# Decay attention beside an FFN on one Trainium2 core: attention's steps in two turns of TensorE per batch, and an earlier, wider spread for one block

## The chip, the cores and the metric

One core of one Trainium2 chip runs the kernel. Its engines work at the same time, each through its own queue in order: TensorE (PE, with weight loads as PEld), VectorE (DVE), ScalarE (ACT), GpSimd (POOL) and SyncE (SP), which issues most DMAs. The metric is device time in microseconds (us), the median over runs.

## The reference

Three stages follow each other; everything is fp32.

```python
# attention with decay: batch 4, heads 8, 768 tokens, head size 48
for t in range(S):
    cur = einsum('bhd,bhe->bhde', u * k[t], v[t])
    y[t] = einsum('bhd,bhde->bhe', r[t], state + cur)
    state = w * state + einsum('bhd,bhe->bhde', k[t], v[t])
x = y as (3072 tokens, 384)
x = (silu(x @ w_gate) * (x @ w_val)) @ w_out          # first FFN, 1536 wide
h = x @ w_in                                          # second FFN, 2048 wide
out = (h * tanh(softplus(h))) @ w_out
```

## The kernel before, in words

The tokens are cut into six blocks j of 128 tokens per batch; a block holds 4 batches b, so 512 columns. Attention works on one (j, b) at a time in chunk form: scores inside the chunk (`at_scores`, L444), a mask copied into an SBUF tile on VectorE (`at_mask`, L451), the output from state and scores (`at_out`, L460 and L468), the sum with the token's own part (`at_y`, L489), the chunk's contribution to the state (`at_state`, L502), the addition into the state (`at_sum`, L518), and a transpose of the output into the FFN's layout (`at_flip`, L539), which ScalarE copies to the high part x_hi (L540) and VectorE subtracts for the low part x_lo (`at_low`, L544). Decay factors (`at_decay`, L392), key factors (`at_keys`, L434) and the own part (`at_own`, L417 to L426) are prepared one batch ahead, from block 2 on mostly by GpSimd.

Every FFN product is three matmuls of split operands (`product`, L227 to L229). A unit is one block times one 128-wide slice of the first FFN: nine matmuls for gate, nine for val and nine of out, which belong to the unit before. Units 0 to 13 alternate between blocks 0 and 1; 14 to 18 finish block 0, 19 to 23 block 1; from unit 24 on come blocks 2 to 5, twelve units each. A string of `UNITS` says in which order a unit is written: "gate", "val" and "out" are matmuls, "act" is ScalarE's silu, "mul" is VectorE's product (L618), "rest" is VectorE's low part g_lo (L626), "tick" is one step of splitting the stored weights (VectorE L144 to L163, the subtraction L185 on VectorE for weights below number 36 and on GpSimd above, ScalarE L136 and L179, SP's loads), and "fill" is a place for attention.

A `Filler` spreads a list of steps evenly over a number of such places; when the next one begins, what is left of the old one is done at once (`flush`). `beside` says at which unit which list begins: at 14 the keys of block 1, at 15 its state updates (8 steps over 8 places), at 19 (`ready`) the two steps of `NEXT` and the 22 of block 2 over 14 places, and at 24, 36 and 48 the 22 steps of blocks 3, 4 and 5 over 34 places. `STEPS` holds the five steps of a batch; the parts of a step are written one after the other into all queues. "back0" is the flip of the batch before, "low1" its low part, "load0" allocates and loads the batch after next. Ticks are handed out at 1.5 a unit in units 14 to 18, at 0 in 19 to 23 and at 1.3 from 24 until all weights are split.

PSUM tiles named "at" (scores, two of them; flip; out; state) take turns on three buffers. The scores, masks and outputs of blocks 0 and 1 are done ahead of unit 0 and the change doesn't touch them.

Of the kernel before, what the change touches and what calls it, by code (L numbers as in the profile page):

```python
# [38 lines left out]


STEPS = [
    "scores0 own0", "mask0 back0 own1", "out0 low1 decay0 own2", "y0 state0 decay1 keys0",
    "sum0 load0",
]
LAST = ["flip0", "low2"]

# [2 lines left out]
NEXT = [[(1, B - 1, "own0 own1 decay1")], [(1, B - 1, "own2 decay0 keys0")]]  # L49


UNITS = [
    "gate act val tick mul tick",
    "gate rest val act tick out mul tick",
    "gate tick rest val act fill tick out mul",
    "gate rest fill act val mul tick out fill tick fill tick",
    "gate rest fill act val mul fill tick out fill tick tick",
]
# [4 lines left out]
PAIRED = 7  # L63
# [5 lines left out]
def tile_decay_attention_then_two_ffns(  # L69
# [31 lines left out]
    class Weights:  # L101
# [92 lines left out]
        def tick(self):  # L194
            n = self.at
            self.size(n + 2)
            self.bits(n)
            self.top(n)
            self.done(n - 2)

            self.load(n + 3)
            if n + 5 < 3 * NF1:
                self.load(n + 4)
                self.load(n + 5)
            self.at += 1
# [386 lines left out]
    def at_steps(j):  # L592

        return [[(j, b, step)] for b in range(B) for step in STEPS + LAST * (b + 1 == B)]
# [9 lines left out]
    def ffn1_mm(j, f, which):  # L604
        hi, lo = xs[j, "x"]
        ps = ps_mm.tile([P, NB], F32, name="mm")
        wt = weights.until((1, f, which))
        for c in range(KC):
            product(ps, wt, cols(c), hi[:, c, :], lo[:, c, :], c == 0, c == KC - 1)
        return ps  # L610

    def ffn1_act(ps):
        sg = opool.tile([P, NB], F32, name="o")
        nc.scalar.activation(sg, ps, AF.Silu)  # L614
        return sg

    def ffn1_gate(j, f, sg, ps):
        nc.vector.tensor_tensor(out=sg, in0=ps, in1=sg, op=ALU.mult)  # L618
        hi = gpool.tile([P, NB], F32R, name="g_hi")
        nc.scalar.activation(hi, sg, AF.Copy)  # L620
        gs[j, f] = [sg, hi]

    def ffn1_rest(j, f, eng):
        sg, hi = gs[j, f]
        lo = gpool.tile([P, NB], F32R, name="g_lo")
        eng.tensor_tensor(out=lo, in0=sg, in1=f32(hi), op=ALU.subtract)  # L626
        gs[j, f] = [hi, lo]

    def ffn1_out(j, f, first, last):
        acc = accs  # L630
        if (j, f) in BESIDE:

            acc = besides
        if first:
            for m in range(KC):
                if acc is besides:
                    acc[m] = ps_at.tile([P, NB], F32, name="at")
                else:
                    acc[m] = ps_acc.tile([P, NB], F32, name=f"acc{m}")
        hi, lo = gs.pop((j, f))  # L640
        wt = weights.until((1, f, 2))
        for m in range(KC):
            product(acc[m], wt, cols(m), hi, lo, first, last)
        if last:
            for m in range(KC):
                o = opool.tile([P, NB], F32, name="o")
                if m == 1:
                    nc.vector.tensor_copy(o, acc[m])
                else:
                    nc.scalar.activation(o, acc[m], AF.Copy)  # L650
                rows = mid[j][:, m * NB : (m + 1) * NB]
                if j in begun:
                    nc.gpsimd.dma_start(out=rows, in_=o, accum_op=ALU.add)
                else:
                    nc.sync.dma_start(out=rows, in_=o)
            begun.add(j)
# [79 lines left out]
    def ending():  # L736
        at_flip(*early[-1])
        at_low(*early[-1])

    def unit1(n, fill=nothing, tick=nothing):  # L740

        j, f, _, _ = units[n]
        gate = val = act = None
        for part in UNITS[n if n < 2 else 2 if n < 2 * PAIRED else 3 if n < 24 else 4].split():
            if part == "gate":
                gate = ffn1_mm(j, f, 0)
                if n == 0:
                    ending()
            elif part == "val":
                val = ffn1_mm(j, f, 1)  # L750
            elif part == "act":
                act = ffn1_act(gate)
            elif part == "mul":
                ffn1_gate(j, f, act, val)
            elif part == "rest" and n:
                ffn1_rest(*units[n - 1][:2], nc.vector)
            elif part == "out" and n:
                ffn1_out(*units[n - 1])
            elif part == "fill":
                fill()  # L760
            elif part == "tick":
                tick()
# [3 lines left out]
    ready = NF1 + PAIRED  # L766
    beside = {
        2 * PAIRED: (KEYS, 3),
        2 * PAIRED + 1: (STATES, 8),
        ready: (NEXT + at_steps(2), 14),  # L770
    }
    beside.update({12 * j - 12: (at_steps(j), 34) for j in range(3, NJ)})
    fill = Filler([], 1)
# [1 line left out]
    for n in range(len(units) - NF1):  # L775
        if n in beside:
            fill.flush()
            fill = Filler(*beside[n])
        due += 2 if n < 2 * PAIRED else 1.5 if n < ready else 0 if n < 24 else 1.3
        some = int(due) if weights.at < W_STORED + 2 else 0  # L780
        ticks = [weights.tick if i < some else nothing for i in range(3)]
        due -= int(due)
        turn = iter(ticks)
        unit1(n, fill, lambda: next(turn)())
# [33 lines left out]
    for f in range(NF1):  # L818
        unit1(len(units) - NF1 + f)
        if f == 2:  # L820
            load_mid(0)
        if f in (5, 6, 7):
            split_mid(0, f - 5)
        for n in range(3 if f else 0):
            weights.tick()
# [186 lines left out]
```

## Time and profile before

| | us |
|---|---|
| median of 3 runs | 957.14 (957.1 to 957.28) |
| profiled execution | 956.94 |
| its span | 955.2 |
| TensorE busy | 944.3 (99% of the span) |
| VectorE, ScalarE, GpSimd busy | 628.2, 473.8, 163.5 |

The busy times are shares of one span, added up over stages of different kinds. A timeline row gives the start of an operation (or of several merged ones, with their count), its length, engine, line and the tiles it writes and reads; in brackets stands how long the engine had been idle before it and what ended that. Matmuls overlap: the distance between two starts tells the time that one takes.

### The profile page before, as it was taken

How to read it: one execution, taken by the hardware profiler on the slowest of the kernel's cores; microseconds unless marked ns; L12 is line 12 of the kernel's file. 1: busy time of each engine (PE TensorE's matmuls, PEld its weight loads, DVE VectorE, ACT ScalarE, POOL GpSimd, SP SyncE). 2: the span in 40 equal slices, each digit the busy share in tenths (PEclk: the TensorE clock that was granted, in tenths of full speed). 3: DMA queues.
4: the chain of work that ended last, by engine and by line, in shares of the span. 5: the costliest groups of instructions: out<-in, count | busy, mean ns of one | idle time of the engine just before them, and what ended most of it. 6: DMA issues, size and time to landing. Idle time of an engine off the chain costs nothing.

```text
span 955.2 us, 14700 instructions
## 1 busy us (share of the span) xinstructions
PE 944.3 (99%) x5707; PEld 770.6 (81%) x5707; DVE 628.2 (66%) x1170; ACT 473.8 (50%) x841; POOL 163.5 (17%) x148
## 2 busy tenths in 40 slices
PE   8999999999999999999999999999999999999998
PEld 6778888787788787888888888888888888888886
DVE  8998868446765766533322249868678777787774
ACT  2455543323343433311221248867676776777673
POOL 5100001764654464322000000000000000000000
PEclk9999999999999999999999999999999999999999
DMA  8464432446646655230046630001001010000000
GB/s 324 176 195 133 132 101 66 128 128 173 218 148 208 217 164 192 92 103 1 1 165 198 197 102 22 12 26 41 1 34 34 0 47 21 1 34 1 33 1 34
DMA packets 35781, 93.17 MB, mean 98 GB/s; under 512 B 4224, under 2 KB 4352, under 8 KB 35712
## 3 DMA queue, kind: packets, MB, share of 16 engines
q1 hardware_dynamic: 35280, 91.44, 29.5%
q0 software_dynamic: 432, 0.79, 0.6%
q8 instruction: 45, 0.74, 0.3%
q14 instruction: 24, 0.20, 0.1%
HBM read 69.41 MB, written 22.81 MB: 97 GB/s over the span
## 4 chain that ended last, share of the span: by engine, by line
PE 87%; DVE 5%; DMA 4%; issue 2%; ACT 1%; POOL 1%; SPq 0%; DVEq 0%; POOLq 0%; ACTq 0%
PE mm L227 12%; PE mm L228 11%; PE mm L229 11%; PE acc L227 11%; PE acc L228 11%; PE acc L229 11%; PE at L228 5%; PE at L229 4%; PE at L227 4%; DMA w_split<-rk_t 2%; PE at L468 2%; PE at L444 2%; PE at L460 1%; DVE w_num L150 1%; DVE w_num L144 1%
## 5 line engine op out<-in xcount | busy, mean ns | idle before, releaser
L227 PE MATMUL mm<-x_hi,w_split 128*128 128x512 f32 x546 | 217.6, 398 | 0.0
L229 PE MATMUL mm<-x_hi,w_split 128*128 128x512 f32 x546 | 213.0, 390 | 0.0
L228 PE MATMUL mm<-x_lo,w_split 128*128 128x512 f32 x546 | 212.9, 390 | 0.0
L228 PE MATMUL acc<-g_lo,w_split 128*128 128x512 f32 x483 | 188.4, 390 | 0.8 <-DVE g_lo L626 0.7
L227 PE MATMUL acc<-g_hi,w_split 128*128 128x512 f32 x483 | 188.8, 391 | 0.0
L229 PE MATMUL acc<-g_hi,w_split 128*128 128x512 f32 x483 | 188.0, 389 | 0.0
L618 DVE TENSOR_TENSOR o<-mm,o 128x512 f32<-128x512 f32 x72 | 49.7, 691 | 192.4 <-PE mm L229 162.4
L227 PEld LDWEIGHTS mm<-x_hi,w_split 128*128 128x128 f32 x546 | 102.5, 188 | 22.7 <-DVE o L618 0.4
L229 PEld LDWEIGHTS mm<-x_hi,w_split 128*128 128x128 f32 x546 | 102.5, 188 | 21.8
L228 PEld LDWEIGHTS mm<-x_lo,w_split 128*128 128x128 f32 x546 | 102.6, 188 | 20.0
L620 ACT ACTIVATE g_hi<-o 128x512 fp32r<-128x512 f32 x72 | 45.5, 632 | 141.4 <-DVE o L618 141.1
L228 PEld LDWEIGHTS acc<-g_lo,w_split 128*128 128x128 f32 x483 | 90.7, 188 | 21.0 <-DVE g_lo L626 2.0
L227 PEld LDWEIGHTS acc<-g_hi,w_split 128*128 128x128 f32 x483 | 90.6, 188 | 19.2
L229 PEld LDWEIGHTS acc<-g_hi,w_split 128*128 128x128 f32 x483 | 90.7, 188 | 18.8
L614 ACT ACTIVATE o<-mm 128x512 f32<-128x512 f32 x72 | 42.8, 594 | 89.5 <-PE mm L229 82.4
L848 ACT ACTIVATE e<-h 128x512 f32<-128x512 f32 x96 | 60.0, 626 | 53.4 <-DVE h L842 50.4
L855 ACT ACTIVATE e<-e 128x512 f32<-128x512 f32 x96 | 59.6, 621 | 49.4 <-DVE e L852 49.3
L862 DVE TENSOR_TENSOR h<-h,e 128x512 f32<-128x512 f32 x96 | 60.0, 687 | 20.5 <-ACT e L861 20.5
L185 POOL TENSOR_TENSOR w_raw<-w_num,w_raw 128x384 fp32r<-128x384 f32 x32 | 40.9, 1279 | 160.4 <-ACT w_raw L179 158.3
L227 PE MATMUL at<-x_hi,w_split 128*128 128x512 f32 x174 | 67.7, 389 | 0.0
L228 PE MATMUL at<-x_lo,w_split 128*128 128x512 f32 x174 | 67.7, 389 | 0.0
L229 PE MATMUL at<-x_hi,w_split 128*128 128x512 f32 x174 | 67.7, 389 | 0.0
(105 smaller groups left out, 1347.6 us busy)
## 6 DMA issues: line engine op xcount, KB each, us to landing
w_raw<-w SPq DMA_DIRECT2D x68, 384.0 KB, 3.5
w2s<-w_raw SPq DMA_DIRECT2D x32, 384.0 KB, 3.7
w_split<-w2s SPq DMA_DIRECT2D x32, 384.0 KB, 3.5
n_sb<-rkv_n SPq DMA_DIRECT2D x16, 576.0 KB, 4.9
rk_sb<-rk_t SPq DMA_DIRECT2D x16, 512.0 KB, 4.5
mid<-o SPq DMA_DIRECT2D x18, 256.0 KB, 2.2
rows<-mid SPq DMA_DIRECT2D x18, 256.0 KB, 2.6
y<-o SPq DMA_DIRECT2D x18, 256.0 KB, 2.3
```

The lines of the kernel that those rows point to most:

```text
L185: eng.tensor_tensor(out=t[:, 1, :], in0=num, in1=f32(t[:, 0, :]), op=ALU.subtract)
L227: nc.tensor.matmul(acc, lhsT=wt[:, 0, sl], rhs=hi, start=start, stop=False)
L228: nc.tensor.matmul(acc, lhsT=wt[:, 0, sl], rhs=lo, start=False, stop=False)
L229: nc.tensor.matmul(acc, lhsT=wt[:, 1, sl], rhs=hi, start=False, stop=stop)
L444: nc.tensor.matmul(ps[g][:, i, :], lhsT=a["k"][q, i, :], rhs=a["r"][q, i, :], start=True, stop=True,)
L468: nc.tensor.matmul(ps[t, h * D : (h + 1) * D], lhsT=scores[h % 2][:, h // 2, t], rhs=a["v"][:, h, :], start=(j == 0 and h == heads[0]), st ...
L614: nc.scalar.activation(sg, ps, AF.Silu)
L618: nc.vector.tensor_tensor(out=sg, in0=ps, in1=sg, op=ALU.mult)
L620: nc.scalar.activation(hi, sg, AF.Copy)
L848: nc.scalar.activation(es[n], hs[n], AF.Exp)
L855: nc.scalar.activation(e, e, AF.Ln, bias=1.0)
L862: nc.vector.tensor_tensor(out=hs[n], in0=hs[n], in1=es[n], op=ALU.mult)
```

## The change

The five steps of a batch are cut anew: the flip of the batch before stands in front of the scores, the low part right behind the mask, the state update right behind the output, its sum behind y, and the load alone. Units 2 and 3 are written in the order that only unit 1 had. The list with block 2's steps begins at unit 17 instead of 19 and is spread over 20 places instead of 14.

```diff
 STEPS = [
-    "scores0 own0", "mask0 back0 own1", "out0 low1 decay0 own2", "y0 state0 decay1 keys0",
-    "sum0 load0",
+    "back0 scores0 own0", "mask0 low1 own1", "out0 state0 decay0 own2",
+    "y0 sum0 decay1 keys0", "load0",
 ]
 LAST = ["flip0", "low2"]
...
-        for part in UNITS[n if n < 2 else 2 if n < 2 * PAIRED else 3 if n < 24 else 4].split():
+        for part in UNITS[0 if n == 0 else 1 if n < 4 else 2 if n < 2 * PAIRED else 3 if n < 24 else 4].split():
...
-        ready: (NEXT + at_steps(2), 14),
+        ready - 2: (NEXT + at_steps(2), 20),
```

## Rows read from the trace of the kernel before

**Rows 1.** The page, part 1: busy us, share of the span, instructions.
```profile
PE 944.3 (99%) x5707; PEld 770.6 (81%) x5707; DVE 628.2 (66%) x1170; ACT 473.8 (50%) x841; POOL 163.5 (17%) x148
```

**Rows 2.** Waits of TensorE: us in total, times, longest us.
```profile
PE at L460 <- DVE s L451: 1.6, 4, 0.5
...
PE acc L228 <- DVE g_lo L626: 0.7, 1, 0.7
```

**Rows 3.** Timeline of VectorE in unit 2: start us, length us, operation.
```profile
58.38 0.35 DVE L144 TENSOR_SCALAR w_num<-w_num 128x384 f32<-128x384 f32 x1
...
60.32 0.68 DVE L626 TENSOR_TENSOR g_lo<-o,g_hi 128x512 fp32r<-128x512 f32 x1
```

**Rows 4.** Timeline of TensorE in unit 2, the out's first two matmuls.
```profile
60.05 0.39 PE L227 MATMUL at<-g_hi,w_split 128*128 128x512 f32 x1
61.06 0.50 PE L228 MATMUL at<-g_lo,w_split 128*128 128x512 f32 x1 [0.62 <-DVE g_lo L626]
```

**Rows 5.** TensorE, block 3: turns alone; the scores stand between the last two.
```profile
240.53 0.39 PE L229 MATMUL mm<-x_hi,w_split 128*128 128x512 f32 x1
240.84 0.88 PE L460 MATMUL at<-state,rk_sb 128*64 128x96 f32 x16
...
244.75 0.39 PE L227 MATMUL mm<-x_hi,w_split 128*128 128x512 f32 x1
...
246.88 0.56 PE L502 MATMUL at<-n_sb 128*48 128x48 f32 x16
...
249.55 0.39 PE L227 MATMUL acc<-g_hi,w_split 128*128 128x512 f32 x1
...
256.99 0.39 PE L227 MATMUL acc<-g_hi,w_split 128*128 128x512 f32 x1
```

**Rows 6.** TensorE, units 19 to 23 (attention of block 2), first and last.
```profile
163.84 0.39 PE L227 MATMUL mm<-x_hi,w_split 128*128 128x512 f32 x1
...
202.47 0.49 PE L539 MATMUL at<-ident,y 128*128 128x128 f32 x3
202.89 0.88 PE L460 MATMUL at<-state,rk_sb 128*64 128x96 f32 x16
...
206.95 0.40 PE L229 MATMUL mm<-x_hi,w_split 128*128 128x512 f32 x1
...
209.59 0.39 PE L227 MATMUL acc<-g_hi,w_split 128*128 128x512 f32 x1
...
211.63 0.39 PE L227 MATMUL mm<-x_hi,w_split 128*128 128x512 f32 x1
```

**Rows 7.** VectorE: a tick of unit 18, and one operation of another.
```profile
162.92 1.16 DVE L144 TENSOR_SCALAR w_num<-w_num 128x384 f32<-128x384 f32 x1
...
166.66 0.55 DVE L163 SCALAR_TENSOR_TENSOR w_num<-w_raw,w_num 128x384 uint32<-128x384 uint32 x1
...
284.05 0.55 DVE L150 SCALAR_TENSOR_TENSOR w_num<-w_raw,w_num 128x384 uint32<-128x384 uint32 x1
```

**Rows 8.** GpSimd beside the first of these ticks, and beside the other.
```profile
162.84 1.03 POOL L417 TENSOR_TENSOR pr<-n_sb 128x384 f32<-128x384 f32 x1
...
284.01 2.62 POOL L426 TENSOR_TENSOR n_sb<-n_sb,bonus 128x384 f32<-128x384 f32 x1 [4.37 <-DVE bonus L425]
```

**Rows 9.** VectorE by line, 170 to 212: busy us, mean ns, idle before.
```profile
L451 DVE COPY_PREDICATED s<-mask,at 128x512 f32<-128x512 uint16 x8 | 5.4, 731 | 6.2 <-PE at L444 6.2
...
L518 DVE TENSOR_TENSOR state<-at,state 48x192 f32<-48x192 f32 x8 | 2.8, 351 | 0.1
L618 DVE TENSOR_TENSOR o<-mm,o 128x512 f32<-128x512 f32 x4 | 2.8, 691 | 13.0 <-issue 6.9 <-PE mm L229 6.1
L489 DVE TENSOR_TENSOR y<-at,n_sb 128x384 f32<-128x384 f32 x4 | 2.2, 554 | 1.0 <-PE at L468 1.0
L544 DVE TENSOR_TENSOR x_lo<-at,x_hi 128x384 fp32r<-128x384 f32 x4 | 2.2, 544 | 0.9 <-ACT x_hi L540 0.9
```

**Rows 10.** TensorE, block 3's batch 2: one of the waits for the mask.
```profile
261.96 0.88 PE L460 MATMUL at<-state,rk_sb 128*64 128x96 f32 x16 [0.36 <-DVE s L451]
```

## The prediction

> **What bounds the kernel now.** I read the busy times first [rows 1]: TensorE is busy for 944.3 of 955.2 us, so the time moves only with what TensorE executes, what it pays for changing between kinds of matmul, and the few waits that it has. The list of its waits comes next [rows 2]; the reader is to see there that no wait on a DMA or on ScalarE is named, that attention's output matmuls (L460) wait four times for the mask, and that the FFN waits for a low part (g_lo). Last come the timelines: of TensorE for what one turn costs [rows 5, 6], of VectorE and GpSimd for how the two disturb each other [rows 7, 8]. The profiled execution took 956.94 us, 1.7 more than its span; it is 0.2 below the median, 957.14. The sum is made on 956.94.
>
> I call a stop of the FFN's matmuls for attention a turn. Nine FFN matmuls in a row take 2.04 (209.59 to 211.63 in [rows 6]), one 0.227. A turn costs what a stretch takes beyond its FFN matmuls.
>
> **Turns alone** [rows 5]: out (O) 244.75 - 240.53 less ten matmuls: 1.95. State (St) 4.80 less eighteen: 0.72. Scores (S) 7.44 less twenty-seven: 1.32. From [rows 6], flip (F) 209.59 - 206.95 less ten: 0.37.
>
> **Turns joined** [rows 6]: O and St back to back start at 202.89, and the eighth start after their first FFN matmul is 206.95: 4.06 less 1.81 is 2.25, with O's lead (240.84 - 240.53 - 0.23 = 0.08) 2.33, against 1.95 + 0.72 = 2.67. A join of O and St is worth 0.34. F followed by attention matmuls takes 0.42 (202.47 to 202.89), and F with S then 0.42 + 1.32 - 0.08 = 1.66 against 1.69: worth 0.03. So of the two joins only one pays. I take bounds of 0.2 to 0.4 and 0 to 0.2 for them.
>
> **Part 1, units 2 and 3 take UNITS[1].** In unit 2 a weight tick (VectorE 58.38 to 60.32, 1.94) stands ahead of the rest that makes g_lo [rows 3], and TensorE's second matmul of the out comes 1.01 after the first instead of 0.23 [rows 4]: 0.8. Behind the change the rest runs where that tick ran, done at about 59.0, before 60.05. The tick is not saved, it moves to the end of the unit: units 3 and 4 then have two ticks in a row ahead of unit 4's rest, some 2 us later than now; by adding the steps of 1.94 and 0.6 it is done at 71.5, its matmul due at 72.8, so nothing is late next. SP's loads and GpSimd have no other work there. -0.8 (bounds -1.0 and 0, if a later rest takes the wait over).
>
> **Part 2, the last state update of block 1.** The filler is flushed at unit 17, so the fourth state follows the third without FFN between: one lead and tail less, -0.2 (0 to -0.4). Its sum stands ahead of a rest that is not needed for 4 us.
>
> **Part 3, block 2.** The 24 steps now run at 14 places of units 19 to 23, 1.7 a place, so that several share a stop. Units 19 to 23 last 47.79 [rows 6], less 135 matmuls (30.6): 17.2 for turns and waits. With 20 places, step s stands at the first place n with 20 s < 24 n. Counted out: batch 0 has S in unit 17's second place, O with St in unit 18's first; batch 1 F with S in unit 18's third, O with St in unit 19's second; batch 2 F, S, mask and low in unit 20's second place and O with St in its third, with no FFN matmul between; batch 3 has two free turns; the last F is alone. Without waits but for batch 2: 1.32 + 2.33 + 1.66 + 2.33 + 1.66 + 2.33 + 0.37 = 12.0. Batch 2: out takes the third buffer of "at" after F's own, so it now waits until low has read F's, and low stands behind both masks: 0.42 + 1.10 + 1.3 + 0.5 + 0.1 + 2.25 = 5.7, with mask, low, sum, mul and y of 0.6 to 0.7 a half, 0.5, 0.7, 0.65 and 0.5 [rows 9]. Together 17.7, so +0.5: before, the mask, O and St shared a stop too.
>
> Then two waits that the start at unit 17 makes, since units 17 and 18 still carry three ticks (units 19 to 23 none).
> First: from the end of unit 17's val, VectorE has mul, tick, tick, mask: 0.6 + 1.94 + 1.94 + 1.3 = 5.8. TensorE has out, S, gate and the first half of O (some 0.7 of the 0.88 in [rows 10]): 2.04 + 1.32 + 2.04 + 0.7 = 6.1, and then needs the mask. That just fits, if a tick takes 1.94. GpSimd, however, gets from unit 17's first place the keys of batch 0 and own and decay of batch 1, whose data lie there since the front, and runs them without a gap. Where that was so, the four VectorE operations of a tick took from 162.92 to 167.2 [rows 7] beside GpSimd's stream [rows 8], 4.2 instead of 1.5: +2.7, so a wait of 2.4. From the other side, at 284.01 [rows 8] it was GpSimd's operation that took 2.62 instead of about 1, and VectorE's L150 beside it kept its 0.55 [rows 7]: a wait of 0. I take 2.3, because unit 17's tick meets a stream that already runs, as at 162.92. Behind the mask on VectorE stand rest and the bonus reduce; their users come later.
> The Trainium skill, page "SBUF — State Buffer", section "Who interferes with whom", says that issue order, not the shape of the operation, decides which of VectorE and GpSimd blocks. Both rows agree with that; by it the sum is 960.4 if GpSimd's stream is there first, 957.6 if the tick is (rival B).
> Second: in unit 18's third place F needs y, and S the buffer that sum gives back. y and sum were put in at the second place, behind mul and a tick: from val's end 0.65 + 1.5 + 0.5 + 0.7 = 3.4 until S may start, against out's 2.04 and F's 0.42. F waits 0.7, S 0.3: 1.0 at least, 1.9 with one GpSimd operation (0.9) in the tick. I take 1.5.
> Block 2: 0.5 + 2.3 + 1.5 = +4.3 (bounds 0.5 + 0 + 1.0 = +1.5 and 0.5 + 2.7 + 1.9 = +5.1).
>
> **Part 4, blocks 3 and 4** (22 steps over 34 places, the step of n at place 17 n / 11). O and St join, eight times. The price is the same buffer: O waits for low behind both masks, where it now waits for the first half of the mask: about 0.65 + 0.45 = 1.1 later wherever VectorE is behind. Of the four waits of [rows 2], one each lies in blocks 3 (261.96, [rows 10]) and 4. There the join saves nothing, as F's 0.37, which lay inside the wait, is now ahead of it: +1.1 each. In block 3, batch 0, sum (0.7) comes ahead of the ticks that already make out wait 0.7 for g_lo [rows 2]; the 0.34 of its join goes there: 0. Block 3: 0 - 0.37 + 1.1 - 0.37 = +0.3; block 4: three clean joins and one wait, 0. Bounds -1.5 and +1.5 each.
> Block 5 has no state: three joins of F, -0.1. The load alone in its step stays at its place; state is read earlier, so SP's two issues wait no longer. Low needs ScalarE's copy of F, a place earlier now: nothing.
>
> **Sum**: -0.8 - 0.2 + 4.3 + 0.3 + 0 - 0.1 = +3.5: 956.94 + 3.5 = **960.4 us**.
>
> **Rivals.**
> (A) Faster: VectorE is nowhere late. GpSimd gives way as at 284.01, and both waits of L460 in blocks 3 and 4 go, because the changed order shifts the ticks against GpSimd's stream. All joins then count: -0.8 - 0.2 + (0.5 + 0 + 1.0) - 1.45 - 1.45 - 0.1 = -2.5: 954.4. For it: the two waits are 0.36 and 0.5 long and two of eight. Against it: low adds 0.5 to the same queue. It decides if a tick in unit 17 stays under some 2.2 us.
> (B) GpSimd gives way in unit 17 alone: the first wait is 0 and the second 1.0: +0.7, 957.6.
> (C) Unit 17 waits as forecast, but blocks 3 and 4 are clean: 3.5 - 0.3 - 2.9 = +0.3, 957.2.
> (D) More waits than forecast: low takes another 1.1 in two of the six clean outs of blocks 3 and 4: 962.6.
>
> **How the numbers follow.** Forecast 0.35, D 0.1, B 0.2, C 0.13, A 0.22. A measurement of this kernel tells 0.2% (1.9 us) from nothing: faster is below 955.2, slower above 959.05. A is faster, B and C no change, the forecast and D slower: 0.22, 0.33, 0.45. The range, 954.4 to 962.6, reaches from A to D since both signs hold a good part; the forecast's own range is 958.8 to 961.8.
>
> **What would show it.** Unit 2's out without an idle before its second matmul (part 1). St right behind O in blocks 3 and 4, with 2.33 for both (joins). In unit 18 an L468 idle for the mask of about 2 us, VectorE's ticks before it drawn out to 4 us; an idle of L539 for y in unit 18's third place; an O in unit 20 that starts some 1.9 after S. In blocks 3 and 4 L460 waiting for x_lo (L544) instead of s (L451). If units 17 and 18 hold no idle on TensorE, the forecast is wrong in its largest term; if TensorE's joined turns take 2.67, the gain of the joins is.

## The result and the profile after

The changed kernel is slower: 963.79 us median of six runs (960.17 to 965.11), against 957.21 of six runs before on the same chip; ratio 1.0056, 95% interval 1.0040 to 1.0072. By this ratio the change costs 5.4 us; the two medians are 6.6 apart. The sign is that of the forecast (+3.5, 960.4), the median lies 1.2 above the range's upper end. The profiled execution is the slowest of the six, 965.11; its span is 963.4, 8.2 more than before.

The page's first part and TensorE's waits, which answer to [rows 1] and [rows 2]:

```profile
PE 946.0 (98%) x5707; PEld 776.1 (81%) x5707; DVE 632.2 (66%) x1170; ACT 474.0 (49%) x841; POOL 163.1 (17%) x148
```
```profile
PE at L460 <- DVE s L451: 3.3, 3, 1.7
PE at L468 <- DVE s L451: 2.6, 2, 2.3
PE at L539 <- DVE y L489: 2.5, 3, 1.4
PE mm L227 <- DVE o L618: 2.5, 1, 2.5
```

Two waits of over 2 us are new: L468 for the mask, and a val for VectorE's mul (L618). To place the time I use that mul runs once a unit, 72 times, so its n-th start marks unit n in every trace. The table gives what each stretch lasts more or less than before; "ahead" is the start of unit 0's first matmul against 44.75. Of the 8.2 us of the changed kernel's span 1.9 lie ahead, 6.1 in the units of the table and 0.2 behind them.

| us against before | ahead | units 0 to 13 | 13 to 24 (block 2) | 24 to 36 (block 3) | 36 to 48 (block 4) | 48 to 71 | sum without ahead |
|---|---|---|---|---|---|---|---|
| changed kernel | +1.91 | +2.82 | +5.56 | -1.75 | -0.40 | -0.12 | +6.11 |
| steps alone | +3.25 | 0.00 | +0.62 | -1.90 | -1.57 | -0.12 | -2.97 |
| units 2, 3 alone | +0.33 | -0.90 | +0.01 | +0.11 | -0.26 | +0.01 | -1.03 |
| places alone | +4.75 | +2.93 | +5.16 | -0.19 | -0.05 | 0.00 | +7.85 |
| late loads | -0.04 | -0.91 | +5.56 | -1.94 | -1.59 | -0.12 | +1.00 |
| small matmuls in the wait | +0.25 | +2.69 | +3.62 | -1.39 | -0.49 | -0.12 | +4.31 |
| ticks ahead | +0.05 | +3.14 | +3.24 | +0.23 | -2.21 | -0.12 | +4.28 |
| late loads and ticks ahead | +0.45 | -0.91 | +3.19 | -0.45 | -1.99 | -0.12 | -0.28 |
| steps and units | +1.61 | -0.88 | +0.67 | -1.19 | -1.58 | -0.12 | -3.10 |
| short preparation | +0.81 | +2.91 | +0.16 | -1.21 | -0.46 | -0.10 | +1.30 |
| steps from block 3 on, and units | +0.15 | -0.91 | +0.01 | -1.28 | -1.55 | -0.12 | -3.85 |

The column "ahead" lies in front of all that the change touches, and varies from one execution to the next: in the changed kernel's profile the granted clock was 0.69 between 15 and 20 us, in the profile before 1.00. Such an execution carries up to 4.75 us that no edit explains; the medians carry some of it too.

**What the front lost.** Timelines of the changed kernel around unit 1: GpSimd, VectorE, TensorE, and the windows (from the busy time of PE to its granted clock, the third number from the end).

```profile
50.46 1.02 POOL L417 TENSOR_TENSOR pr<-n_sb 128x384 f32<-128x384 f32 x1 [12.22 <-DMA n_sb<-rkv_n]
51.56 1.01 POOL L419 TENSOR_TENSOR pr<-pr,u_sb 128x384 f32<-128x384 f32 x1
52.52 1.59 POOL L392 TENSOR_TENSOR rk_sb<-rk_sb,tab 128x512 f32<-128x512 f32 x1
```
```profile
50.72 0.98 DVE L144 TENSOR_SCALAR w_num<-w_num 128x384 f32<-128x384 f32 x1
51.62 1.36 DVE L150 SCALAR_TENSOR_TENSOR w_num<-w_raw,w_num 128x384 uint32<-128x384 uint32 x1
52.91 1.62 DVE L185 TENSOR_TENSOR w_split<-w_num,w_split 128x384 fp32r<-128x384 f32 x1
...
55.19 0.68 DVE L618 TENSOR_TENSOR o<-mm,o 128x512 f32<-128x512 f32 x1
```
```profile
55.92 0.80 PE L227 MATMUL mm<-x_hi,w_split 128*128 128x512 f32 x1 [2.48 <-DVE o L618]
56.52 0.63 PE L228 MATMUL mm<-x_lo,w_split 128*128 128x512 f32 x1
56.94 0.63 PE L229 MATMUL mm<-x_hi,w_split 128*128 128x512 f32 x1
```
```profile
56.00:60.00 4.00, 4.00 (x11) 3.18 (x12) 4.00 (x11) 2.47 (x5) 0.00 (x0) 0.61 0.60 168
```

These three GpSimd operations prepare block 2. Before, they stood in GpSimd's queue behind its first weight subtraction, and ran when that did; GpSimd's timeline of before:

```profile
161.87 1.02 POOL L185 TENSOR_TENSOR w_raw<-w_num,w_raw 128x384 fp32r<-128x384 f32 x1 [125.54 <-ACT w_raw L179]
162.84 1.03 POOL L417 TENSOR_TENSOR pr<-n_sb 128x384 f32<-128x384 f32 x1
```

Written two units earlier, they come ahead of it. Nothing in the queue holds them any more, and they run when their data land, at 50 us, where VectorE is behind: its tick lasts from 50.72 to 55.19, 4.5 instead of 1.94 [rows 3]. mul of unit 0 is late, the next val waits 2.48 for the PSUM tile that mul frees, and its matmuls then start 0.43 apart, the lower of the clock's two levels (0.61 is the mean over 4 us), for 3.4 us. It is not the loads that draw out the tick: the kernel before issues them in the same place (43.2 and 44.2, 5.4 and 8.1 us to landing), and its tick at 48.81 takes 1.94.

**What block 2 lost.** The changed kernel's units 17 and 18: GpSimd, VectorE and TensorE, then a window.

```profile
161.37 1.13 POOL L417 TENSOR_TENSOR pr<-n_sb 128x384 f32<-128x384 f32 x1
162.57 1.20 POOL L419 TENSOR_TENSOR pr<-pr,u_sb 128x384 f32<-128x384 f32 x1
163.74 1.61 POOL L392 TENSOR_TENSOR rk_sb<-rk_sb,tab 128x512 f32<-128x512 f32 x1
```
```profile
160.89 0.74 DVE L144 TENSOR_SCALAR w_num<-w_num 128x384 f32<-128x384 f32 x1
...
165.95 0.34 DVE L144 TENSOR_SCALAR w_num<-w_num 128x384 f32<-128x384 f32 x1
...
167.90 1.32 DVE L451 COPY_PREDICATED s<-mask,at 128x512 f32<-128x512 uint16 x2
```
```profile
165.52 0.88 PE L460 MATMUL at<-state,rk_sb 128*64 128x96 f32 x16
168.66 1.95 PE L468 MATMUL at<-n_sb,s 128*64 128x48 f32 x32 [2.26 <-DVE s L451]
...
178.22 0.52 PE L539 MATMUL at<-ident,y 128*128 128x128 f32 x3 [0.80 <-DVE y L489]
```
```profile
168.00:176.00 8.00, 7.34 (x61) 6.26 (x62) 2.80 (x5) 2.06 (x6) 3.98 (x4) 0.57 0.15 57
```

The first tick takes 5.06 (160.89 to 165.95), the second 1.95, the mask is late and L468 waits 2.26: this is the forecast's first wait, to 0.04 of its size. The second is there too, 0.80. But behind the first the clock was at the lower level for 6.7 us (0.57 in the mean over 8 us), which the forecast did not have.

### The profile page after: what moved, and what is told of

Same layout as the page of the kernel before. It is cut to its first block, busy times and chain, and to the rows that moved or that the text cites. A ratio compares the mean times of both kernels' runs of the same rounds, so it can differ in the third digit from the quotient of the medians.

```text
span 963.4 us, 14692 instructions
## 1 busy us (share of the span) xinstructions
PE 946.0 (98%) x5707; PEld 776.1 (81%) x5707; DVE 632.2 (66%) x1170; ACT 474.0 (49%) x841; POOL 163.1 (17%) x148
## 4 chain that ended last, share of the span: by engine, by line
PE 89%; DVE 4%; DMA 2%; issue 1%; ACT 1%; POOL 0%; SPq 0%; DVEq 0%; POOLq 0%; ACTq 0%
PE mm L227 12%; PE mm L228 12%; PE mm L229 12%; PE acc L228 11%; PE acc L227 11%; PE acc L229 11%; PE at L229 4%; PE at L227 4%; PE at L228 4%; PE at L468 2%; PE at L444 1%; PE at L460 1%; DMA w_raw<-w 1%; PE at L539 1%; DVE w_num L150 1%
## 5 line engine op out<-in xcount | busy, mean ns | idle before, releaser
L618 DVE TENSOR_TENSOR o<-mm,o 128x512 f32<-128x512 f32 x72 | 49.7, 691 | 194.1 <-PE mm L229 165.3
L614 ACT ACTIVATE o<-mm 128x512 f32<-128x512 f32 x72 | 42.8, 594 | 97.1 <-PE mm L229 89.0
L876 DVE TENSOR_TENSOR g_lo<-h,g_hi 128x512 fp32r<-128x512 f32 x96 | 65.6, 686 | 2.2
```

Of the source, the lines that this page charges most:

```text
L876: nc.vector.tensor_tensor(out=lo, in0=h, in1=f32(hi), op=ALU.subtract)
```

## The experiments

Theory P, formed on the two traces: the early start of block 2's list costs everything, through GpSimd's preparation at 50 us and in units 17 and 18; the steps and the units gain. Its rival S: the closer order of mask, low, output and state costs.

**The three edits alone.** Each is one hunk of the diff above.

> The new steps alone, places and units as before. Theory P (the early start of block 2's list costs everything: GpSimd's preparation for block 2 becomes the first thing in its queue, runs at about 50 us beside the weight ticks, and again meets the ticks of units 17 and 18): faster, about 955.0 (957.2 less 1.8 in block 3 and 0.4 in block 4), no wait of TensorE over 1 us behind 45 us. Theory S (the closer order of mask, low, output and state makes TensorE wait): 959 or more, with waits of L460 or L468 over 1 us in units 19 to 23.

> The order of units 2 and 3 alone. Forecast's part 1: 956.4 (0.8 less), no wait for g_lo in unit 2. Rival (the wait moves to a later unit): 957.2 with a g_lo wait in unit 3 or 4.

> Block 2's list from unit 17 over 20 places alone, steps and units as before. Theory P: slower by 6 to 8, 963 to 965: a val in unit 1 waits 2 to 3 for its PSUM tile with the clock at its lower level behind it (3.6 together), and unit 18's output waits about 2 for the mask with the lower clock behind it. Theory S: within 1 of before, 956 to 958.

Steps alone: 956.78, ratio 0.9987 (0.9976 to 0.9997). Units alone: 956.53, 0.9985 (0.9971 to 0.9999), -0.90 in units 0 to 13 and no wait for g_lo there. Places alone: 964.21, 1.0072 (1.0051 to 1.0092), with the same two waits:

```profile
PE at L468 <- DVE s L451: 2.6, 2, 2.3
PE mm L227 <- DVE o L618: 2.5, 1, 2.5
```

S falls: with the old steps the places cost all of it, and the new steps gain. The steps' median gain, 0.6, is smaller than the 2.2 expected; the profile has 2.97 behind the first unit and +3.25 ahead of it, so most of the difference lies where the edit does nothing.

**Block 2's first loads later.** In the changed kernel the four DMAs that bring the data of block 2's first two batches are issued in front of unit 16.

```diff
-    for b in range(2):
-        at_tiles(EARLY, b)
-        load_at(EARLY, b)
...
     for n in range(len(units) - NF1):
...
+        if n == 16:
+            for b in range(2):
+                at_tiles(EARLY, b)
+                load_at(EARLY, b)
```

> The changed kernel with block 2's first two loads issued ahead of unit 16 instead of ahead of unit 0, so that GpSimd cannot begin at 50 us. Theory P: the wait near 55 us and the lower clock behind it go, 960.2 (963.8 less 3.6); the wait in unit 18 stays. Rival (the wait near 55 us comes from the new order of units 2 and 3 or from the weights' loads): the wait stays, 963.8.

959.86, ratio 1.0022 (1.0007 to 1.0037), 3.9 below the changed kernel: expected was 3.6. GpSimd now starts behind the DMA:

```profile
145.98 1.39 POOL L417 TENSOR_TENSOR pr<-n_sb 128x384 f32<-128x384 f32 x1 [109.71 <-DMA n_sb<-rkv_n]
```

Units 0 to 13 gain 0.91 instead of losing 2.82, and the windows at 50 to 60 us have the full clock. The front's loss is thus shown: 3.73 for the wait and the clock behind it.

Block 2 again costs 5.56, but that the sum is the same is chance. GpSimd's stream now covers the whole first tick of unit 17, which takes 6.31 (155.20 to 161.51), and the output waits longer:

```profile
164.22 1.28 PE L468 MATMUL at<-n_sb,s 128*64 128x48 f32 x32 [3.52 <-DVE s L451]
```

In return the clock is at the lower level for 3.4 us (165.4 to 168.8) instead of 6.7.

**TensorE kept busy in the wait.** Between the two halves of block 2's first output, 24 small matmuls write to the tile's unused columns; they disturb the sums of that tile, so this output is not the kernel's.

```diff
+WARM = 24
...
+        for _ in range(WARM if (j, b) == (EARLY, 0) else 0):
+            nc.tensor.matmul(ps[:, DM:], lhsT=mask, rhs=mask, start=True, stop=True, skip_group_check=True)
         heads = [*range(0, H, 2), *range(1, H, 2)]
```

> The changed kernel with 24 small matmuls on unused columns between the two halves of block 2's first output, where TensorE idles 2.3 for the mask. Theory C (the idle brings TensorE's clock to its lower level and that costs 3 more): the mask still comes at the same time, but the matmuls behind it run at 0.227 apart, about 961 (963.8 less 3). Rival (they are slow for another reason, or the clock falls in any case): 0.43 apart as before, 963.8 or more.

961.27, ratio 1.0035 (1.0023 to 1.0047). The timeline, L467 being the small matmuls, L471 the second half and L542 the next flip, and a window:

```profile
164.54 1.51 PE L467 MATMUL at<-mask 128*128 128x128 bf16 x24
166.86 1.29 PE L471 MATMUL at<-n_sb,s 128*64 128x48 f32 x32 [0.81 <-DVE s L452]
...
174.49 0.52 PE L542 MATMUL at<-ident,y 128*128 128x128 f32 x3 [1.67 <-DVE y L492]
```
```profile
166.00:174.00 8.00, 6.01 (x67) 4.75 (x66) 5.57 (x11) 3.22 (x9) 4.19 (x4) 1.00 0.15 59
```

The mask comes as late as it did, the clock stays at 1.00, and block 2 loses 3.62 instead of 5.56. So the lower clock cost block 2 1.9. By the rows alone it is 3.0 (in the changed kernel L468 and state took 2.52 and the nine FFN matmuls behind them 4.00; at batch 1's turn, 186.98 to 190.53, it was 1.38 and 2.17). Most of the difference comes back in the flip, which now waits 1.67 for y instead of 0.80.

**Ticks ahead of unit 17**, alone and with the late loads.

```diff
-        due += 2 if n < 2 * PAIRED else 1.5 if n < ready else 0 if n < 24 else 1.3
+        due += 2 if n < ready - 2 else 1 if n == ready - 2 else 0 if n < 24 else 1.3
```

> The changed kernel with the weight ticks of units 14 to 18 dealt out 2, 2, 2, 1, 0 instead of 1, 2, 1, 2, 1. Theory P (ticks of units 17 and 18 meet GpSimd's stream and hold mask and y back): the wait of L468 in unit 18 falls to 0.5 or less, the lower clock behind it and the flip's wait for y go, 958.5 to 959.5; the wait near 55 us stays. Rival (the mask is late because of the steps or of GpSimd itself): L468 waits 2 as before, 963.8.

> The changed kernel with the late loads and the ticks dealt out 2, 2, 2, 1, 0: both collisions away. Theory P: 954 to 956, since the steps and units then show their gain. Rival (GpSimd's work, now in units 15 and 16 beside two ticks each, makes a new wait there): 958 or more with a wait in units 15 to 17.

The first was a miss: 962.35, ratio 1.0043 (1.0020 to 1.0067). L468's wait fell to 0.3 and the flip's to 0.2, but others came instead:

```profile
PE mm L227 <- ACT o L614: 2.9, 2, 2.2
PE mm L227 <- DVE o L618: 2.6, 1, 2.6
PE acc L228 <- DVE g_lo L626: 2.5, 2, 2.1
```

The 2.1 (2.09 at 162.15, in unit 17's out) and another wait of 0.75 (155.47, unit 17's first matmul) lie where the moved ticks now stand: VectorE comes to its rest only behind two ticks and the sums, and ScalarE's L614 of unit 16 stands behind the tick's L179, which waited until L502 was done (154.40). The 2.2 lies elsewhere, at 236.28, the start of unit 26 in block 3: there ScalarE's L614 runs only at 235.63, behind a DMA from its buffer to mid. Why that came later than in the changed kernel was not followed.

With the late loads it is 959.84, ratio 1.0007 (0.9982 to 1.0033): no different from before, and above the 954 to 956 expected. The rival held here: the waits of 0.75 and 2.07 in unit 17 are there again (151.75 and 158.44), one of 1.51 at the start of unit 26 too, and block 2 again loses 3.19. In neither of the two spreads that were run do the seven ticks of units 14 to 18 fit beside block 2's early start.

**GpSimd's preparation cut short.** Batch 1's own part and decay and the last own operation of batch 0 work on a few columns only, so their results are left undone; the ticks stay.

```diff
+SHORT = {(2, 0, 2), *((2, 1, i) for i in (0, 1, 2, 4, 5))}
...
+        if (j, b, 4 + i) in SHORT:
+            eng.tensor_tensor(out=junk, in0=t[:, 0, :8], in1=tabs[i][:, 0, :8], op=ALU.mult)
...
+        n = 4 if (j, b, i) in SHORT else D
```

The last line is in `at_own`, whose operands are all cut to n of the 48 columns.

> The changed kernel with GpSimd's preparation for block 2's batch 1 (own part and decay, five operations) and the last own operation of batch 0 cut to a few columns each; their results are left undone. The ticks stay in units 17 and 18. Theory P (GpSimd's stream draws out the tick of unit 17 and so holds the mask): that tick takes about 2 instead of 4.6 us, L468 in unit 18 waits less than 0.5, the clock stays, and block 2 costs 3 to 5 less, 959 to 961. Rival (the two ticks and the mask are too much for VectorE without GpSimd): L468 waits 1 or more, 963.8 less at most 1.

958.48, ratio 1.0004 (0.9990 to 1.0019). VectorE's ticks and mask, and TensorE's output (L474 and L482 are its halves, L553 the flip):

```profile
159.87 0.35 DVE L145 TENSOR_SCALAR w_num<-w_num 128x384 f32<-128x384 f32 x1
...
161.88 0.34 DVE L145 TENSOR_SCALAR w_num<-w_num 128x384 f32<-128x384 f32 x1
...
163.83 1.35 DVE L465 COPY_PREDICATED s<-mask,at 128x512 f32<-128x512 uint16 x2
```
```profile
164.50 0.88 PE L474 MATMUL at<-state,rk_sb 128*64 128x96 f32 x16
165.21 1.09 PE L482 MATMUL at<-n_sb,s 128*64 128x48 f32 x32
...
171.80 0.41 PE L553 MATMUL at<-ident,y 128*128 128x128 f32 x2 [0.84 <-DVE y L503]
```

With the same ticks in the same units, the first tick takes 2.01 instead of 5.06, L482 follows L474 without a wait, the clock stays, and block 2 costs 0.16 instead of 5.56, a little more gained than the 3 to 5 expected. So 5.4 of block 2's loss hang on GpSimd's operations beside the ticks. The Trainium skill's rule that I had weighed ("SBUF — State Buffer", section "Who interferes with whom") says that issue order, not the shape of the operation, decides which of the two engines blocks. The changed kernel's trace agrees with it twice: GpSimd's operations began ahead of VectorE's tick, at 50.46 against 50.72 and at 160.39 against 160.89, and the tick was drawn out. In the second case of [rows 8] the order was the other way: the tick began at 283.78 with L144, GpSimd's operation at 284.01, and that one was drawn out.

**Towards a faster version.** Steps and units with the old places; then with block 2 on the old steps as well (`OLD if j == EARLY else STEPS` in `at_steps`).

> New steps and the order of units 2 and 3, with block 2's list as before (from unit 19, 14 places). Theory P, by adding the two runs of the parts alone: ratio 0.9972 or less, 954.5, and from the first unit on 4.0 less than before in the profile. Rival (the parts disturb each other): 956 or more.

> New steps for blocks 3 to 5 only, block 2 with the old steps from unit 19 over 14 places, and the order of units 2 and 3: the parts that gained, without those that lost. Theory P, from the profiles of the parts (units 2 and 3 -1.0, block 2 0, blocks 3 to 5 -3.6): 4 to 4.6 less behind the first unit, ratio 0.9955 to 0.997. Rival (block 2's own order is not what cost 0.6 in the run of the steps alone): as the run of steps and units together, ratio 0.998.

Steps and units: 955.86, ratio 0.9980 (0.9967 to 0.9994), a smaller gain than the 954.5 expected; behind the first unit its profile gains 3.10 instead of 4.0. The mixed version: **954.37**, ratio 0.9973 (0.9954 to 0.9992), the lowest median of all, 3.3 below before on its chip, with the full clock in its profile. Its interval overlaps that of steps and units, so the times alone do not tell the two apart; the profiles do, in block 2. In 14 places several steps share a stop. In the old order the flip lies between scores and output and fills part of the wait for the mask; in the new it lies ahead of the scores, and the output waits. Block 2's second output in the version with new steps, then in the mixed one (L464 is the output, L448 the scores, L543 the flip):

```profile
181.05 0.49 PE L539 MATMUL at<-ident,y 128*128 128x128 f32 x3
181.47 1.16 PE L444 MATMUL at<-rk_sb 48*128 48x128 f32 x16
183.45 0.88 PE L460 MATMUL at<-state,rk_sb 128*64 128x96 f32 x16 [0.82 <-DVE s L451]
```
```profile
179.66 1.16 PE L448 MATMUL at<-rk_sb 48*128 48x128 f32 x16
180.75 0.55 PE L543 MATMUL at<-ident,y 128*128 128x128 f32 x3
181.63 0.88 PE L464 MATMUL at<-state,rk_sb 128*64 128x96 f32 x16 [0.34 <-DVE s L455]
```

The version with new steps has two such waits (0.82 and 0.81), the mixed one waits 0.34 at both. In sum block 2 costs 0.67 in the first and 0.01 in the second.

## Why the prediction was right in sign and short in size

Part 1, units 2 and 3 (-0.8): right, -0.90 in the run of the units alone. In the changed kernel itself it is hidden under the front's loss.

Part 2, block 1's last state (-0.2): its unit, 17, came 0.36 earlier; within its bounds.

Part 3, block 2 (+4.3, with part 2's -0.2 4.1; measured 5.56). The place and the cause of the first wait were right, shown by the short preparation. Its size agrees too (2.3, measured 2.26), but that close only by luck: the tick was drawn out by 3.1, not 2.7, while L468 waited for the first half of the mask alone, 0.76 behind the mask's start, where the sum had both halves, 1.3. The mis-sized term of this part comes behind the wait: there TensorE ran at the lower clock, 3.0 in the rows and 1.9 net, which the sum had at 0. The second wait was put at 1.5 and is 0.80, because the slower val let GpSimd finish (174.3) before unit 18's tick began (176.06). In the run with small matmuls, at the full clock, that tick met a GpSimd operation (171.55) and took 2.30 instead of 1.47, and the wait was 1.67. Batch 2 in unit 20 was put at 5.7; from the last FFN matmul ahead of it (194.39) to the tenth start behind it (201.27) it takes 6.88 less 2.27, 4.6. There my claim about the buffer failed: the output starts at 197.01, when the first half of the mask is through, and low runs only at 197.47:

```profile
196.23 1.37 DVE L451 COPY_PREDICATED s<-mask,at 128x512 f32<-128x512 uint16 x2 [2.71 <-PE at L444]
197.47 0.56 DVE L544 TENSOR_TENSOR x_lo<-at,x_hi 128x384 fp32r<-128x384 f32 x1
```
```profile
197.01 0.88 PE L460 MATMUL at<-state,rk_sb 128*64 128x96 f32 x16 [0.81 <-DVE s L451]
```

So out does not wait for the buffer that the flip had, here or in blocks 3 and 4, where all its waits are for the mask (L451), none for low (L544). Counting allocations by threes was wrong.

Part 4, blocks 3 and 4 (+0.3 and 0; measured -1.75 and -0.40, and -1.90 and -1.57 with the steps alone). The join is what was forecast: output and state in one turn,

```profile
249.81 0.39 PE L229 MATMUL mm<-x_hi,w_split 128*128 128x512 f32 x1
250.12 0.88 PE L460 MATMUL at<-state,rk_sb 128*64 128x96 f32 x16
...
251.75 0.53 PE L502 MATMUL at<-n_sb 128*48 128x48 f32 x16
252.21 0.50 PE L227 MATMUL acc<-g_hi,w_split 128*128 128x512 f32 x1
...
254.39 0.39 PE L227 MATMUL mm<-x_hi,w_split 128*128 128x512 f32 x1
```

254.39 - 249.81 less ten matmuls is 2.31, where I had 2.33 and where [rows 5] make 2.67 of two turns. What failed is the price set against it, 1.1 in each block for the same buffer of low that out does not use. With it gone the blocks come to -1.45 each by my own joins, the clean case of rival A, and that is about what the steps alone show. In the changed kernel block 4 has one long wait for the mask, 1.66 at 342.03, where the steps alone wait 0.55. The two ticks ahead of that mask take 7.35 in the changed kernel, beside GpSimd operations without a gap, and 5.42 with the steps alone, where GpSimd has a gap of 1.05; that this is the cause was not tested by a run.

The step that was left out altogether is the front, +3.73. Part 1 has it that GpSimd has no other work there, and in part 3 I had written that GpSimd's data lie there since the front, and that it runs its preparation without a gap, but followed this queue only from unit 17 on. What stood ahead of these operations in GpSimd's queue, and that they would lose it, was to be read from its timeline of before, where the first operation behind 36 us is a weight subtraction at 161.87. So three terms were off: +3.7 missed, +1.9 of the clock missed, and some -3 of waits that did not come. The sum of the profile without the stretch ahead, +6.1, is 2.6 above the forecast's +3.5.

The right sign is thus in good part luck. Without the front and the clock, which the forecast did not have, some +0.4 is left (6.11 less 3.73 and 1.94). That is next to rival C (unit 17 waits, blocks 3 and 4 are clean: +0.3), which would have been no change. Rivals A and B fell with unit 17's tick, which took 5.06. D fell with the buffer: no O waited for low. None of the rivals had the front or the clock.

## What to carry to other kernels

An instruction written earlier in an in-order queue does not run where it is written but as soon as what stood ahead of it is gone: look at what held it, and at which engine it will meet at the time when its data land. An idle of TensorE of some 2 us can cost more than its own length: here a stretch of 3.4 to 6.7 us at the lower clock followed some of them and not others, so the forecast needs both cases. A closer order of small steps pays by the lead and the tail of a turn (0.34 here) only where the engine between them has time.

## What was unexpected of the hardware

Behind two idles of the changed kernel, of 2.48 and 2.26 us, the granted clock was at its lower level for 3.4 and 6.7 us; with the late loads it was there for only 3.4 us behind an idle of 3.52. Behind an idle of 1.66 (342.03) it did not fall, nor, in the kernel with the ticks ahead, behind those of 2.09 and 2.19. Filling 1.5 us of the wait in unit 18 with small matmuls kept it at 1.00. What decides between these cases is open. And the first 25 us differ between the profiled executions, by up to 4.75 us of instructions that no edit touches, with the clock between 15 and 20 us anywhere from 0.5 to 1.0; that is nearly as much as the change itself, so edits of 1 us show in the profiles by stretch before they show in the medians.
